# Batch 0 of a local-attention and token-mixing kernel: theta's weight jobs queued behind later softmax groups, half of the token weights queued behind theta, spare tiles and ScalarE steps for theta

## Chip, cores and metric

The kernel runs on one core of a Trainium2 chip. The metric is the device time of one launch in microseconds. The engines are TensorE (PE, with PEld for its weight loads), VectorE (DVE), ScalarE (ACT), GpSimd (POOL), and SyncE (SP), which issues all the transfers here.

## What is computed

For each of four batches (576 tokens, 8 heads of 64 channels):

```
scores = q @ k.T / 8, masked: head 0-3 see the last 32 tokens,
         head 4-7 see every 4th of the last 128
x      = softmax(scores) @ v                  # heads side by side: 576 x 512
theta  = x @ w_theta                          # 512 x 512
zr, zi = x * cos(theta), x * sin(theta)
u      = x + w_tok_r @ zr + w_tok_i @ zi      # mixes the 576 tokens
x2     = u + relu(u @ w_ch)
h      = relu(x2 @ w_in); hu, hv = halves of h
out    = (hu * (w_spatial @ layernorm(hv) + b)) @ w_out
```

Queries, keys and values come in single precision, all the weight matrices in double precision. A product of two single-precision matrices is computed as three passes of reduced-precision matmuls: each operand is split into a high part and the remainder (names ending in `h` and `l`), and high*high, low*high and high*low are added up.

## The kernel before

**Weights.** A weight piece comes in as 64-bit numbers, and the engines put together a single-precision value from them (`bits64`, lines 115 to 134): one scaling on ScalarE (L128) or POOL (L130), then three integer steps on DVE (L131 to L133). `split_weight` (L136) then writes the high part (L107 on ScalarE, L109 on DVE, L111 on POOL) and the remainder (L144, on POOL or DVE). There are four buffers for the 64-bit input (`w`) and four for the value (`w64g`). theta's weights are four jobs of two halves, all on POOL but for the DVE steps (`THETA_ENG`, L55; `w_theta_job`, L159). The token weights `wtok` have nine row blocks (k) and two column halves (c), so 18 jobs: half c=0 uses ScalarE, ScalarE and POOL, half c=1 POOL, POOL and DVE (`TOK_ENG`, L53).

**Attention.** One batch is 12 groups (`groups`, four head pairs of three). For a group, `att_scores` (L215) computes the scores, adds the mask on TensorE in batch 0 (L231), takes the maximum on DVE (L245 in batch 0; L249 and L250 in later batches), the exponentials on ScalarE (L253), one over their sum on DVE (L254, L255), and multiplies on POOL (L256). Two steps later `att_transpose` transposes the result, four steps later `att_values` multiplies with the values and ScalarE copies the result into `x`. The loads of all four head pairs of batch 0 are issued at its start (`att_load`, L195); the first two pairs of batch 1 are loaded behind the last transfer of token half c=0.

**Theta.** `th_unit` (L323) handles 128 tokens; the units of batch 0 run in the order 4, 0, 1, 2, 3 (unit 4 has the last 64 tokens). It scales and splits x on DVE (`xh` L335, `xl` L336), makes 12 matmuls (L341), rounds on ScalarE (`ta`, L345), subtracts on DVE (L346), transposes x (L349), takes the absolute value on DVE (`tb`, L350), two sines on ScalarE (L351, L352), two products with x on DVE (L355; L362 and L363 for unit 4), and splits each product: `zh` on DVE (L109) or POOL (L111), `zl` on POOL (L316). `ta` and `tb` have two buffers each, and unit 4's products use one of `ta`. A buffer comes free when POOL has read the product for `zl`.

**Mixing.** `tm_run` (L388) multiplies `z` by `wtok`, in 27 matmuls for each of four channel blocks and two token halves (column half c of `wtok`). The first two channel blocks of half c=0 are built up together, k by k, as the units of theta are done (L404); the rest at L411.

**Order.** Each engine carries out its instructions in order. A planner sets that order when the kernel is built: it goes by program order as the priority and by a model of when each instruction's operands are ready. The program order around the change is set by `spread`, which weaves jobs into a main sequence at a rate, and by `behind` (L480), which adds the rule that what a job issues on ScalarE, DVE and POOL comes after given instructions of the same engine. Before the change:

```
spread(attention(0), (jobs(j_theta), W_RATE0))
spread(th_run(0, (4, 0, 1, 2, 3)), (jobs([lambda f=f: behind(f) for f in j_tok0]), 2.0))
for b in range(PAIR):
    spread(chain(tm_run(b, K_ALL), take(ch, CH_BEFORE)), (attention(b + 1), ATT_RATE),
           (take(second, 12) if b else jobs(j_tok1 + j_ch), ...))
```

So theta's weight jobs are woven into attention of batch 0 with nothing that holds them; the jobs of token half c=0 are held behind the last softmax group of batch 0; the jobs of c=1 are written after theta and held by nothing; attention of batch 1 is woven into the mixing of batch 0.

Of the kernel before, what the change touches and what calls it, by code (L numbers as in the profile page):

```python
# [11 lines left out]
F32 = mybir.dt.float32  # L12
# [27 lines left out]


LAG_T, LAG_V = 2, 4
W_RATE0 = 0.5
TOK_RATE = 2.25
ATT_RATE, ATT_RATE_PAIR = 2.0, 3.0
TAIL_RATE = 1.0
# [16 lines left out]
def tile_block(ctx: ExitStack, tc: tile.TileContext, qT, kT, vw, eye_in, mask_in, eye_b_in, w_theta, w_tok, w_ch, w_in, w_sp, w_sph, b_sp, w_out, out):  # L63
# [3 lines left out]
    def f32(ap):  # L67
        return ap.bitcast(F32)
# [87 lines left out]
        split_weight(src[:, k, cs], t[:, 0], t[:, 1], *engs)  # L156
        SY.dma_start(f32(dst[:, k, :, cs]), f32(t))

    def w_theta_job(k):  # L159
        halves(w_theta, wth_h, wth_l, k, DM, THETA_ENG)  # L160

    def w_tok_job(k, c):
        cs = slice(CH * c, CH * (c + 1))
# [22 lines left out]
        for j in range(2):  # L186
            G.memset(qz[D * (1 - j):D * (2 - j), j], 0.0)

    last_softmax = {}
    tok0_dma = []  # L190
    groups = [(b, hp, g) for b in range(B) for hp in range(4) for g in range(3)]
    att = {}
# [2 lines left out]
    def att_load(b, hp):  # L195
        early = b == 0 and hp >= 2
        qz = qz_2[hp - 2] if early else qzero[hp % 2]
        kt = kt_2[:, hp - 2] if early else patt.tile([P, S + WIN], F32, tag="k", name="kt", bufs=2)
        first = b == 0 and hp == 0
        n = KW + (NA - 1) * T  # L200
        for c0, c1 in ((0, n), (n, S + WIN)) if first else ((0, S + WIN),):
            SY.dma_start(kt[:, c0:c1], kT[b, hp, :, c0:c1])
            if c0 == 0:
                SY.dma_start(qz[:D, 0], qT[b, hp, :D])
            if first and c0 == 0:
                SY.dma_start(masks, mask_in)
                SY.dma_start(eye_b, eye_b_in)
        SY.dma_start(qz[D:, 1], qT[b, hp, D:])
        if first:
            SY.dma_start(ident, eye_in)  # L210
        vt = vt_2[:KW, hp - 2] if early else patt.tile([KW, NT, P], F32, tag="v", name="vt", bufs=2)
        SY.dma_start(vt, vw[b, hp])
        heads[b, hp] = (qz, kt, vt, {})

    def att_scores(m):  # L215

        b, hp, g = groups[m]
        if g == 0 and (b or not hp):

            with tc.issue_after(tok0_dma[-1].ins) if b == 1 and hp < 2 else nullcontext():  # L220
                for h in range(1 if b else 4):
                    att_load(b, hp + h)
        if hp == 0 and g == 0:
            x[b] = p1.tile([P, 4, S], F32, tag="x", name=f"x{b}", bufs=2)
        qz, kt, vt, pT = heads[b, hp]
        s = ps_mm.tile([P, 512], F32, tag="mm", name="s")
        kind = 2 * (hp // 2) + g // 2
        on_pe = b < PE_MASK
        def mask_half(first):
            if on_pe:  # L230
                PE.matmul(s[:, :3 * KW], eye_b, masks[:, kind].rearrange("p t k -> p (t k)"), start=first, stop=not first)  # L231

        mask_half(True)
        for i in range(2 * 3):
            blk, h = i // 2, i % 2
            o = s[T * h:T * (h + 1), KW * blk:KW * (blk + 1)]
            j, t = (g, i) if g < 2 else (h, NA + blk)
            PE.matmul(o, qz[:, j, T * t:T * (t + 1)], kt[:, T * t:T * t + KW], start=not on_pe, stop=not on_pe)  # L238
        mask_half(False)
        sm = patt.tile([P, 3, KW], F32, tag="sm", name="sm", bufs=5)  # L240
        m_ = patt.tile([P, 3], F32, tag="m", name="m", bufs=3)
        l = patt.tile([P, 3], F32, tag="l", name="l", bufs=3)
        sv = s[:, :3 * KW].rearrange("p (t k) -> p t k", t=3)
        if on_pe:
            V.tensor_reduce(m_, sv, op=ALU.max, axis=AX.X, negate=True)  # L245
            A.mul(m_, m_, D**-0.5)
            src, scale = sv, D**-0.5
        else:
            V.scalar_tensor_tensor(sm, sv, D**-0.5, masks[:, kind], op0=ALU.mult, op1=ALU.add)  # L249
            V.tensor_reduce(m_, sm, op=ALU.max, axis=AX.X, negate=True)  # L250
            src, scale = sm, 1.0
        for t in range(3):
            ia = A.activation(sm[:, t, :], src[:, t, :], AF.Exp, bias=m_[:, t:t + 1], scale=scale, accum_out=l[:, t:t + 1])  # L253
        V.tensor_scalar_add(l, l, 1e-9)  # L254
        iv = V.reciprocal(l, l)  # L255
        ig = G.tensor_tensor(sm, sm, l.unsqueeze(2).to_broadcast([P, 3, KW]), op=ALU.mult)  # L256
        last_softmax[b] = (ia, iv, ig)
        att[m] = sm

    def att_transpose(m):  # L260
# [48 lines left out]


    zh, zl = {}, {}
    uu = {}

    def split(dst_h, dst_l, src, eh="a", el="g"):
        copy(dst_h, src, eh)
        (G if el == "g" else V).tensor_tensor(dst_l, src, f32(dst_h), op=ALU.subtract)  # L316

    def ztile(k, bufs=1):
        h = pz.tile([P, DM], F32R, tag=f"zh{k}", name=f"zh{k}", bufs=bufs)
# [3 lines left out]
    def th_unit(b, t, pair=False):  # L323
# [8 lines left out]
        h = pth.tile([P, 4, P], F32R, tag="xh", name="xh", bufs=2)[:, :, :n]  # L332
        l = pth.tile([P, 4, P], F32R, tag="xl", name="xl", bufs=2)[:, :, :n]

        V.tensor_scalar(h, src, INV2PI, None, op0=ALU.mult)  # L335
        V.scalar_tensor_tensor(l, src, INV2PI, f32(h), op0=ALU.mult, op1=ALU.subtract)  # L336
        ps = ps_mm.tile([P, 512], F32, tag="mm", name="ps_th")[:n]
        i = 0
        for k in range(4):
            for lh, rh in ((h, wth_h), (l, wth_h), (h, wth_l)):  # L340
                PE.matmul(ps, lh[:, k, :], rh[:, k, :], start=(i == 0), stop=(i == 11))  # L341
                i += 1
        ta = pth.tile([P, DM], F32, tag="ta", name="ta", bufs=2)[:n]
        tb = pth.tile([P, DM], F32, tag="tb", name="tb", bufs=2)[:n]
        A.activation(ta, ps, AF.Identity, bias=magic[:n, 0:1])  # L345
        V.scalar_tensor_tensor(ta, ta, MAGIC, ps, op0=ALU.subtract, op1=ALU.subtract)  # L346
        xn = ps_t.tile([P, 512], F32, tag="pt", name="ps_xn")[:n]
        for k in range(4):
            PE.transpose(xn[:, P * k:P * (k + 1)], src[:, k, :], ident)  # L349
        V.tensor_scalar(tb.bitcast(U32), ta.bitcast(U32), 0x7FFFFFFF, None, op0=ALU.bitwise_and)  # L350
        A.activation(ta, ta, AF.Sin, scale=-TURN)  # L351
        A.activation(tb, tb, AF.Sin, scale=-TURN, bias=half_pi[:n, 0:1])  # L352
        if t < 4:
            for k, tt in ((t, tb), (4 + t, ta)):
                V.tensor_tensor(tt, xn, tt, op=ALU.mult)  # L355
                zh[b, k], zl[b, k] = ztile(k)
                split(zh[b, k], zl[b, k], tt, Z_HI[k // 4], "g")
        else:
            for i in range(2 if pair else 1):
                r_ = slice(HALF * i, HALF * (i + 1))  # L360
                zz = pth.tile([P, DM], F32, tag=("ta", "tb")[i], name="zz", bufs=2)
                V.tensor_tensor(zz[:HALF], xn[r_], tb[r_], op=ALU.mult)  # L362
                V.tensor_tensor(zz[HALF:], xn[r_], ta[r_], op=ALU.mult)  # L363
                zh[b + i, 8], zl[b + i, 8] = ztile(8, 2)
                split(zh[b + i, 8], zl[b + i, 8], zz, "a", "g")

    xs = {}

    def th_keep(b):
# [86 lines left out]
    def jobs(fns):  # L456
        for f in fns:
            f()
            yield
# [6 lines left out]
        for g in gens:  # L466
            yield from g

    j_theta = [lambda k=k: w_theta_job(k) for k in range(4)]
    j_tok0 = [lambda k=k: w_tok_job(k, 0) for k in K_ALL]  # L470
    j_tok1 = [lambda k=k: w_tok_job(k, 1) for k in K_ALL]
    j_ch = [lambda k=k: w_ch_job(k) for k in range(4)]

    H2 = DM // 2
# [2 lines left out]
    j_out = [lambda k=k, c=c: stored(w_out, wo_d, k, slice(H2 * c, H2 * (c + 1)), OUT_ENG) for k in range(4) for c in range(2)]  # L477

    second = jobs(j_in + j_sp + j_out)
    def behind(f):  # L480

        with ExitStack() as st:
            for i in last_softmax[0]:
                st.enter_context(tc.issue_after(i.ins))
            f()
        tok0_dma.append(last_dma[0])

    spread(attention(0), (jobs(j_theta), W_RATE0))
    spread(th_run(0, (4, 0, 1, 2, 3)), (jobs([lambda f=f: behind(f) for f in j_tok0]), 2.0))
    for b in range(PAIR):  # L490
        ch = ch_run(b)
        spread(chain(tm_run(b, K_ALL), take(ch, CH_BEFORE)), (attention(b + 1), ATT_RATE), (take(second, 12) if b else jobs(j_tok1 + j_ch), 1.0 if b else TOK_RATE))
# [303 lines left out]
```

## Time and profile before

| | us |
|---|---|
| median of 3 runs | 570.19 |
| lowest and highest run | 569.38, 571.11 |
| the profiled execution | 569.31 |
| its span, first to last instruction | 567.5 |
| PE, PEld busy in the span | 534.8, 478.4 |
| DVE, ACT, POOL busy in the span | 331.0, 241.9, 262.1 |

The span is the profiled execution without what lies before its first and behind its last instruction. Busy times are of one execution. A wait is put down to the instruction that came last of those waited for. In a chain of waits each line has its start, its length and what it was. DVE's and ScalarE's instructions overlap a little at their ends, so a sum of durations is somewhat over the busy time of a stretch.

### The profile page before, as it was taken

What the parts mean: (1) busy time and instruction counts of PE and PEld (TensorE: products, weight loads), DVE (VectorE), ACT (ScalarE), POOL (GpSimd) and SP (SyncE); (2) the same over time, 40 slices, a digit from 0 to 9 for tenths busy, and PEclk for the clock granted to TensorE, in tenths of its full rate; (3) what the DMA queues carried; (4) which work ended last, traced back from release to release, by engine and by line L of the source; (5) the groups of instructions that cost most, each with busy time, mean ns of one, the idle gap of its engine ahead of it and who ended that gap; (6) DMA issues with size and microseconds to landing.
All of it is one profiled execution on the core that took longest, in us unless ns stands there. A gap on an engine that the chain in (4) does not pass through costs nothing.

```text
span 567.5 us, 11263 instructions
## 1 busy us (share of the span) xinstructions
PE 534.8 (94%) x4148; PEld 478.4 (84%) x4148; DVE 331.0 (58%) x844; ACT 241.9 (43%) x710; POOL 262.1 (46%) x333
## 2 busy tenths in 40 slices
PE   5887689999999999998899999999999999999997
PEld 3665578888988999877888999899899889988996
DVE  3589899898797269747697115773610327354030
ACT  3766476635655435766444212432322224223222
POOL 3484687552995348944349534334211203332040
PEclk9979799999999999999799999999999999999999
DMA  8845636672259453667400799705025110001002
GB/s 213 221 129 171 162 112 181 196 216 82 74 176 263 138 163 106 206 208 233 144 8 33 264 362 381 242 3 167 0 75 164 42 55 1 1 1 68 8 1 94
DMA packets 49935, 76.07 MB, mean 134 GB/s; under 512 B 4052, under 2 KB 30552, under 8 KB 49880
## 3 DMA queue, kind: packets, MB, share of 16 engines
q1 hardware_dynamic: 49880, 75.35, 43.3%
q8 instruction: 33, 0.54, 0.4%
q14 instruction: 22, 0.18, 0.1%
HBM read 52.53 MB, written 22.81 MB: 133 GB/s over the span
## 4 chain that ended last, share of the span: by engine, by line
PE 62%; DVE 10%; DMA 9%; POOL 7%; ACT 5%; issue 5%; SPq 1%; POOLq 0%; DVEq 0%; ACTq 0%
PE ps_y L411 12%; PE ps_sp L671 9%; PE ps_hu L652 9%; PE ps_o L700 9%; PE ps_hv L607 9%; PE ps_r L430 6%; POOL zl L316 2%; DMA wsp_d<-parts 2%; PE ps_th L341 2%; DMA w<-w_theta 1%; PE s L238 1%; DMA kt<-kT 1%; PE pt L266 1%; DVE xl L336 1%; DMA x2d<-parts 1%
## 5 line engine op out<-in xcount | busy, mean ns | idle before, releaser
L411 PE MATMUL ps_y<-wtok_h,zh 128*128 128x288 f32 x270 | 81.8, 306 | 1.7 <-DVE ta L346 0.9
L411 PE MATMUL ps_y<-wtok_h,zl 128*128 128x288 f32 x270 | 81.1, 301 | 0.4 <-POOL zl L316 0.4
L411 PE MATMUL ps_y<-wtok_l,zh 128*128 128x288 f32 x270 | 80.0, 298 | 0.0
L316 POOL TENSOR_TENSOR gl<-hu,gh 128x288 fp32r<-128x288 f32 x32 | 26.0, 811 | 74.6 <-ACT gh L107 74.6
L411 PEld LDWEIGHTS ps_y<-wtok_h,zh 128*128 128x128 f32 x270 | 50.7, 189 | 4.9 <-DVE sm L249 1.3
L675 DVE TENSOR_TENSOR hu<-ps_sp,hu 128x288 f32<-128x288 f32 x32 | 14.6, 455 | 66.8 <-PE ps_sp L674 66.8
L411 PEld LDWEIGHTS ps_y<-wtok_h,zl 128*128 128x128 f32 x270 | 51.0, 189 | 1.9 <-POOL zl L316 0.8
L411 PEld LDWEIGHTS ps_y<-wtok_l,zh 128*128 128x128 f32 x270 | 50.8, 189 | 0.2
L316 POOL TENSOR_TENSOR vl<-hv,vh 128x512 fp32r<-128x512 f32 x16 | 20.9, 1304 | 62.6 <-ACT vh L107 55.2
L256 POOL TENSOR_TENSOR sm<-sm,l 128x288 f32<-128x288 f32 x48 | 32.0, 673 | 31.6 <-DVE l L255 26.0
L253 ACT ACTIVATE sm<-sm,m 128x96 f32<-128x96 f32 x108 | 39.1, 364 | 13.4 <-DVE m L250 9.5
L316 POOL TENSOR_TENSOR ul<-x,uh 128x288 fp32r<-128x288 f32 x32 | 26.4, 832 | 25.2 <-ACT uh L107 25.1
L671 PE MATMUL ps_sp<-wsp_h,vh 128*128 128x288 f32 x128 | 37.8, 296 | 0.0
L430 PE MATMUL ps_r<-uh,wch_h 128*128 128x288 f32 x128 | 37.8, 296 | 0.0
L671 PE MATMUL ps_sp<-wsp_l,vh 128*128 128x288 f32 x128 | 37.8, 296 | 0.0
L671 PE MATMUL ps_sp<-wsp_h,vl 128*128 128x288 f32 x128 | 37.8, 295 | 0.0
L652 PE MATMUL ps_hu<-x2l,win_h 128*128 128x288 f32 x128 | 37.7, 295 | 0.0
L652 PE MATMUL ps_hu<-x2h,win_h 128*128 128x288 f32 x128 | 37.7, 295 | 0.0
L652 PE MATMUL ps_hu<-x2h,win_l 128*128 128x288 f32 x128 | 37.7, 295 | 0.0
L430 PE MATMUL ps_r<-uh,wch_l 128*128 128x288 f32 x128 | 37.7, 296 | 0.0
L316 POOL TENSOR_TENSOR parts<-x,parts 128x288 fp32r<-128x288 f32 x32 | 26.8, 844 | 23.4 <-ACT parts L107 23.4
L430 PE MATMUL ps_r<-ul,wch_h 128*128 128x288 f32 x128 | 37.4, 295 | 0.0
(169 smaller groups left out, 1590.9 us busy)
## 6 DMA issues: line engine op xcount, KB each, us to landing
x2d<-parts SPq DMA_DIRECT2D x32, 288.0 KB, 2.3
vt<-vw SPq DMA_DIRECT2D x16, 432.0 KB, 4.7
w<-w_tok SPq DMA_DIRECT2D x18, 288.0 KB, 2.8
x2h<-x2d SPq DMA_DIRECT2D x8, 576.0 KB, 7.7
x2l<-x2d SPq DMA_DIRECT2D x8, 576.0 KB, 10.9
kt<-kT SPq DMA_DIRECT2D x15, 304.0 KB, 4.5
w<-w_in SPq DMA_DIRECT2D x16, 256.0 KB, 3.5
win_d<-parts SPq DMA_DIRECT2D x16, 256.0 KB, 2.2
```

What stands on the lines that cost most here:

```text
L238: PE.matmul(o, qz[:, j, T * t:T * (t + 1)], kt[:, T * t:T * t + KW], start=not on_pe, stop=not on_pe)
L253: ia = A.activation(sm[:, t, :], src[:, t, :], AF.Exp, bias=m_[:, t:t + 1], scale=scale, accum_out=l[:, t:t + 1])
L256: ig = G.tensor_tensor(sm, sm, l.unsqueeze(2).to_broadcast([P, 3, KW]), op=ALU.mult)
L316: (G if el == "g" else V).tensor_tensor(dst_l, src, f32(dst_h), op=ALU.subtract)
L341: PE.matmul(ps, lh[:, k, :], rh[:, k, :], start=(i == 0), stop=(i == 11))
L411: PE.matmul(ps[:, :CH], lh[b, k][:, P * d:P * (d + 1)], rh[:, k, cs], start=(n == 0), stop=(n == 3 * len(ks) - 1))
L430: PE.matmul(ps[:, :CH], lh[:, k, P * e:P * (e + 1)], rh[:, k, cs], start=(n == 0), stop=(n == 11))
L607: PE.matmul(ps, lh[:, k, ts_], rh[:, k, DM:], start=(n == 0), stop=(n == 11))
L652: PE.matmul(ps[:, :CH], lh[:, k, fs], rh[:, k, cs], start=(n == 0), stop=(n == 11))
L671: PE.matmul(ps[:, :CH], lh[b, k][:, fs], rh[:, k, cs], start=(n == 0), stop=False)
L675: V.tensor_tensor(t[:, f, cs], ps[:, :CH], t[:, f, cs], op=ALU.mult)
L700: PE.matmul(ps, lh[:, k, ts_], rh[:, k, cs], start=(n == 0), stop=(n == 11))
```

## The change

- The masks of batch 0's first group come in a load of their own; the other three kinds follow behind the second half of the first queries.
- theta's weights become eight half jobs. Two are written after attention step 6, two after 7, one after 8, two after 9 and one after 10, and what each issues on ScalarE, DVE and POOL is queued behind that step's softmax.
- In batch 0, `xh` and the absolute value move from DVE to ScalarE.
- Units 0 and 1 of batch 0 use a spare tile for `ta` and `tb`, in the slot that held batch 0's early values and later holds `uh`.
- The nine jobs of token half c=1 are queued behind unit 3 of theta: behind its last sine on ScalarE, its last product on DVE and its last `zl` on POOL.

```diff
-W_RATE0 = 0.5
+TH_FROM, TH_RATE = 6, 6
...
-    def w_theta_job(k):
-        halves(w_theta, wth_h, wth_l, k, DM, THETA_ENG)
+    def w_theta_job(k, c):
+        cs = slice(DM // 2 * c, DM // 2 * (c + 1))
+        split_weight(w_theta[:, k, cs], wth_h[:, k, cs], wth_l[:, k, cs], *THETA_ENG)
...
-                SY.dma_start(masks, mask_in)
+                SY.dma_start(masks[:, :1], mask_in[:, :1])
                 SY.dma_start(eye_b, eye_b_in)
         SY.dma_start(qz[D:, 1], qT[b, hp, D:])
         if first:
+            SY.dma_start(masks[:, 1:], mask_in[:, 1:])
             SY.dma_start(ident, eye_in)
...
-        last_softmax[b] = (ia, iv, ig)
+        softmax[m] = (ia, iv, ig)
...
-        V.tensor_scalar(h, src, INV2PI, None, op0=ALU.mult)
+        if b == 0:
+            A.mul(h, src, INV2PI)
+        else:
+            V.tensor_scalar(h, src, INV2PI, None, op0=ALU.mult)
...
-        ta = pth.tile([P, DM], F32, tag="ta", name="ta", bufs=2)[:n]
-        tb = pth.tile([P, DM], F32, tag="tb", name="tb", bufs=2)[:n]
+        if b == 0 and t in (0, 1):
+            if not t:
+                spare.append(p1.tile([P, 4, DM], F32, tag="uh", name="spare"))
+            ta, tb = (spare[0][:, 2 * t + i, :] for i in range(2))
+        else:
+            ta, tb = (pth.tile([P, DM], F32, tag=g, name=g, bufs=2)[:n] for g in ("ta", "tb"))
...
-        V.tensor_scalar(tb.bitcast(U32), ta.bitcast(U32), 0x7FFFFFFF, None, op0=ALU.bitwise_and)
+        if b == 0:
+            A.activation(tb, ta, AF.Abs)
+        else:
+            V.tensor_scalar(tb.bitcast(U32), ta.bitcast(U32), 0x7FFFFFFF, None, op0=ALU.bitwise_and)
         A.activation(ta, ta, AF.Sin, scale=-TURN)
-        A.activation(tb, tb, AF.Sin, scale=-TURN, bias=half_pi[:n, 0:1])
+        ia = A.activation(tb, tb, AF.Sin, scale=-TURN, bias=half_pi[:n, 0:1])
...
-                V.tensor_tensor(tt, xn, tt, op=ALU.mult)
+                iv = V.tensor_tensor(tt, xn, tt, op=ALU.mult)
                 zh[b, k], zl[b, k] = ztile(k)
-                split(zh[b, k], zl[b, k], tt, Z_HI[k // 4], "g")
+                zlast[b] = ia, iv, split(zh[b, k], zl[b, k], tt, Z_HI[k // 4], "g")
...
-    spread(attention(0), (jobs(j_theta), W_RATE0))
-    spread(th_run(0, (4, 0, 1, 2, 3)), (jobs([lambda f=f: behind(f) for f in j_tok0]), 2.0))
+    for m, _ in enumerate(attention(0)):
+        for i in range(8):
+            if m == TH_FROM + TH_RATE * i // 10:
+                behind(softmax[m], lambda: w_theta_job(i // 2, i % 2))
+    s_last = softmax[11]
+
+    def tok0(k):
+        behind(s_last, lambda: w_tok_job(k, 0))
+        tok0_dma.append(last_dma[0])
+
+    spread(th_run(0, (4, 0, 1, 2, 3)), (jobs([lambda k=k: tok0(k) for k in K_ALL]), 2.0))
+    z_last = zlast[0]
+    j_tok1 = [lambda k=k: behind(z_last, lambda: w_tok_job(k, 1)) for k in K_ALL]
```

## Rows read from the trace of the kernel before

**Rows 1.** Busy time by stretch: PE, PEld, DVE, ACT, POOL, clock, DMA share, GB/s
```profile
0.00:7.00 7.00, 1.28 (x13) 1.03 (x13) 1.17 (x4) 1.28 (x1) 3.57 (x10) 1.00 0.61 169
7.00:24.00 17.00, 15.73 (x204) 10.98 (x203) 7.16 (x25) 12.19 (x68) 4.33 (x7) 1.00 1.01 262
24.00:38.00 14.00, 11.02 (x144) 8.33 (x143) 12.39 (x38) 8.57 (x37) 12.99 (x27) 0.76 0.50 137
38.00:78.00 40.00, 31.02 (x185) 24.24 (x185) 36.26 (x76) 24.00 (x50) 24.96 (x30) 0.91 0.57 154
70.30:78.00 7.70, 7.70 (x76) 7.14 (x77) 7.70 (x18) 7.61 (x18) 6.81 (x10) 0.96 0.49 132
82.00:121.00 39.00, 39.00 (x427) 35.07 (x428) 36.62 (x107) 22.64 (x86) 25.73 (x42) 1.00 0.67 189
```

**Rows 2.** Chain that ended last, 50 to 82 us: start, length, what
```profile
56.06 5.65 DMA w<-w_tok
...
69.87 0.69 ACT ta L345
...
73.39 1.28 ACT L351
```

**Rows 3.** Timeline of DVE and POOL, 58 to 101 us: start, length, what
```profile
61.86 0.44 POOL L130 TENSOR_SCALAR w64g<-w 128x288 f32<-128x288 f32 x1 [2.10 <-DMA w<-w_tok]
...
70.66 0.45 DVE L131 TENSOR_SCALAR c<-w 128x288 uint32<-128x288 uint32 x1
...
77.31 0.68 DVE L355 TENSOR_TENSOR ta<-ps_xn,ta 128x512 f32<-128x512 f32 x1
...
100.85 0.45 DVE L144 TENSOR_TENSOR wtok_l<-w64g,wtok_h 128x288 fp32r<-128x288 f32 x1
```

**Rows 4.** ACT's groups, 38 to 78 us: busy us, mean ns, idle before
```profile
L128 ACT ACTIVATE w64g<-w 128x288 f32<-128x288 f32 x9 | 4.1, 471 | 7.4 <-POOL wtok_l L144 3.3 <-POOL wth_l L144 1.7 <-DMA w<-w_tok 1.2
...
L345 ACT ACTIVATE ta<-ps_th,magic 128x512 f32<-128x512 f32 (+1 forms) x5 | 3.4, 684 | 6.7 <-POOL zl L316 6.6
L351 ACT ACTIVATE ta<-ta 128x512 f32<-128x512 f32 (+1 forms) x5 | 3.2, 631 | 1.7 <-DVE tb L350 1.7
...
L253 ACT ACT_TABLE_LOAD x2 | 2.6, 1283 | 0.0
L253 ACT ACTIVATE sm<-sm,m 128x96 f32<-128x96 f32 x6 | 2.2, 365 | 0.0
L253 ACT ACTIVATION_READ_ACCUMULATOR sm<-sm,m 128x1 f32 x5 | 0.9, 186 | 0.0
```

**Rows 5.** DVE's groups, 38 to 78 us: busy us, mean ns, idle before
```profile
L346 DVE SCALAR_TENSOR_TENSOR ta<-ta,ps_th 128x512 f32<-128x512 f32 (+1 forms) x5 | 3.4, 676 | 2.2 <-ACT ta L345 2.2
...
L350 DVE TENSOR_SCALAR tb<-ta 128x512 uint32<-128x512 uint32 (+1 forms) x5 | 2.6, 525 | 0.0
L335 DVE TENSOR_SCALAR xh<-x 128x512 fp32r<-128x512 f32 (+1 forms) x5 | 2.5, 535 | 0.8 <-ACT x L296 0.8
```

**Rows 6.** Timeline of SP, first 7 us: start, length, what
```profile
1.80 0.58 SPq L206 DMA_DIRECT2D masks<-mask  x1
```

**Rows 7.** Who waited for whom, 7 to 24 us: total us, times, longest
```profile
POOL w64g L130 <- DMA w<-w_theta: 3.9, 1, 3.9
DVE c L131 <- DMA w<-w_theta: 2.7, 1, 2.7
```

**Rows 8.** DVE's groups, 70.6 to 101.4 us: busy us, mean ns, idle before
```profile
L350 DVE TENSOR_SCALAR tb<-ta 128x512 uint32<-128x512 uint32 x1 | 1.0, 977 | 0.0
L346 DVE SCALAR_TENSOR_TENSOR ta<-ta,ps_th 128x512 f32<-128x512 f32 x1 | 0.7, 679 | 0.0
L355 DVE TENSOR_TENSOR ta<-ps_xn,ta 128x512 f32<-128x512 f32 x1 | 0.7, 676 | 0.0
L355 DVE TENSOR_TENSOR tb<-ps_xn,tb 128x512 f32<-128x512 f32 x1 | 0.7, 654 | 0.0
L109 DVE CAST zh<-tb 128x512 fp32r<-128x512 f32 x1 | 0.4, 414 | 0.0
```

More of the change, by code (lines that the diff above doesn't have):

```diff
@@ L187, in tile_block @@
             G.memset(qz[D * (1 - j):D * (2 - j), j], 0.0)
-    last_softmax = {}
+    softmax = {}
     tok0_dma = []
@@ L311, in tile_block @@
     zh, zl = {}, {}
+    zlast = {}
     uu = {}
@@ L315, in split @@
         copy(dst_h, src, eh)
-        (G if el == "g" else V).tensor_tensor(dst_l, src, f32(dst_h), op=ALU.subtract)
+        return (G if el == "g" else V).tensor_tensor(dst_l, src, f32(dst_h), op=ALU.subtract)
     def ztile(k, bufs=1):
@@ L365, in th_unit @@
                 split(zh[b + i, 8], zl[b + i, 8], zz, "a", "g")
+    spare = []
     xs = {}
@@ L467, in chain @@
             yield from g
-    j_theta = [lambda k=k: w_theta_job(k) for k in range(4)]
-    j_tok0 = [lambda k=k: w_tok_job(k, 0) for k in K_ALL]
-    j_tok1 = [lambda k=k: w_tok_job(k, 1) for k in K_ALL]
     j_ch = [lambda k=k: w_ch_job(k) for k in range(4)]
@@ L479, in tile_block, with behind @@
     second = jobs(j_in + j_sp + j_out)
-    def behind(f):
+    def behind(ins, f):
         with ExitStack() as st:
-            for i in last_softmax[0]:
+            for i in ins:
                 st.enter_context(tc.issue_after(i.ins))
             f()
+    for m, _ in enumerate(attention(0)):
[5 more added lines that the diff above has]
+        behind(s_last, lambda: w_tok_job(k, 0))
         tok0_dma.append(last_dma[0])
-    spread(attention(0), (jobs(j_theta), W_RATE0))
-    spread(th_run(0, (4, 0, 1, 2, 3)), (jobs([lambda f=f: behind(f) for f in j_tok0]), 2.0))
+    spread(th_run(0, (4, 0, 1, 2, 3)), (jobs([lambda k=k: tok0(k) for k in K_ALL]), 2.0))
+    z_last = zlast[0]
+    j_tok1 = [lambda k=k: behind(z_last, lambda: w_tok_job(k, 1)) for k in K_ALL]
     for b in range(PAIR):
```

## The prediction

> **What bounds the kernel now.** I read the busy time by stretch first [rows 1]. The reader is to see four stages. From 7 to 24 us the DMA engines are full (share 1.01) and the vector engines mostly wait: the queries, keys and values of batch 0 are arriving. From 24 to 38 us DVE (12.39 of 14 us) and POOL (12.99) are full: the last softmax groups and theta's weights. From 38 to 78 us, batch 0's theta with the first half of the token weights, DVE is full again (36.26 of 40) while TensorE idles 9 us and runs at a mean granted clock of 0.91, so part of it at the lower of its levels of 1.2 and 2.4 GHz. From 82 to 121 us TensorE never stops and DVE has 36.62 of 39 us. So the only stretch that can give time back is the one before 82 us, and whatever the change pushes behind it meets a full TensorE and a nearly full DVE.
>
> Then the chain of waits inside that stretch [rows 2]. It goes from a transfer of token weights of 5.65 us into POOL's first conversion step of the *second* token half (L130 at 61.86, [rows 3]), from there through POOL's queue to ScalarE's L345 at 69.87, and on over a read of ScalarE's table at 73.39. Two faults show. POOL, in order, stands behind a second-half job that theta does not need; and ScalarE's L345 of units 2 and 3 waits 6.6 us in all for POOL's zl (idle column of [rows 4]), because `ta` has two buffers and the one wanted is still read by POOL. DVE in turn stands 2.2 us before its L346 [rows 5].
>
> **The change part by part.** All in the profiled execution's own time, 569.31 us, which lies 0.88 us under the 570.19 us median of the runs shown.
>
> *Masks in two loads.* 72 of 288 KB now go ahead of the small identity for which TensorE's first matmul waits. At 169 GB/s [rows 1] the 221 kB moved back are worth at most 1.3 us; one more issue on SP costs at most the 0.58 us of the present one [rows 6]. I take nothing: the transfers are full from 7 to 24 us, the bytes are the same, and the last of them set the end of that stage. The third group needs the moved part, which comes behind the query half that the group waits for as well.
>
> *Theta's weights behind softmax groups 6 to 10.* The same eight half jobs, so no engine gains work. Now POOL stands 3.9 us and DVE 2.7 us for the first theta weight [rows 7] with softmax work queued behind them. The constraint puts only group 6 ahead of the first two jobs; the job's transfer lands no earlier, because SP issues it behind the same loads, so both engines stand at the next job instead and groups 7 to 11 still queue there. What moves into the gap is one POOL multiply and two short DVE steps, under 1 us. The stage from 24 to 38 us is full on both engines [rows 1]. Bounds: 0 and the whole DVE stand of 2.7 us; I take 0, the nearer by the order.
>
> *ScalarE takes xh and the absolute value.* Five units each: DVE loses 2.5 us (L335, the scaled copy xh) and 2.6 us (L350, the absolute value) [rows 5], 5.1 us. ScalarE gains ten steps. The nearest rows are its own 512-wide ones, 684 and 631 ns [rows 4]: ten times 0.66 is 6.6 us. DVE's L350 and L335 took 0.53 us, so a unit's own latency grows by about 0.25 us; over a pipeline of five units that shows once or twice, under 0.5 us.
>
> The Trainium skill speaks against this part (page "ScalarE: Activation LUTs", section "Rules for kernel authors"): multiplications and the like belong on VectorE, which is faster. The rows agree on the single step (0.53 against 0.66 us); whether it decides here is the second rival below.
>
> *Spare tiles for units 0 and 1.* They remove the wait for POOL's zl: 6.6 us of ScalarE, of which 2.2 us stood on DVE. What is late next is the unit's product with x on DVE, that is, DVE's own queue. The spare space is the slot of batch 0's early value tiles, which attention has read before theta begins, and POOL's last reading of it (unit 1) lies ahead of unit 3, so it is free before the first mixed column is written into that slot; no wait from it.
>
> *Second token half behind theta.* It removes POOL's L130 from in front of zh and 2.1 us of standing there [rows 3]. Nine jobs wait behind unit 3's last product on DVE and last subtraction on POOL; ScalarE has none of their steps. Their transfers are not held, except that the fifth waits for a buffer that the first job frees. That job's first DVE step is at 70.66 now [rows 3], so SP, with the next batch's later loads behind it, is not held longer unless theta ends after that.
>
> **The sum.** When does theta's last DVE product end? Now at 78.0 [rows 3]. From 38 to 78 us DVE is busy 36.26. Away go 5.1 us (moved). Between 70.3 and 78 us DVE is busy all 7.70 us [rows 1], of which unit 3's own steps are 0.98 + 0.68 + 0.65 + 0.68 = 3.0 us [rows 8]; the other 4.7 us, second-half weights and the next batch's softmax, go behind theta. That leaves 26.5 us. With the 3.7 us of idle time of now, the end comes at 38 + 26.5 + 3.7 = 68.2. Dense it would be 64.5; with twice the idle time, since fill work has left DVE, 72.0.
>
> What is that worth? DVE delivers the nine second-half weights from 70.66 to 101.3 us [rows 3], 30.6 us, and TensorE's second column half is woven around them. In these 30.6 us lie 3.4 us of unit 3 (3.0 us and L109's 0.41 [rows 8]). Started on a DVE free of theta they need 27.2 us, so a start at 74.1 us would change nothing, and a start at 68.2 brings everything after it forward by **5.9 us** (9.6 dense, 2.1 with twice the idle). TensorE can follow: it has 9 us of idle time before 78 us and slow stretches besides. After 121 us I expect the same work, shifted. So 563.4 us in profiled time, and 564.3 us as a median of runs.
>
> **Rivals.**
> *Stage one pays too.* If the order that the planner finds leaves groups 7 and 8 ahead of the first theta weight, the 2.7 us that DVE stands there become useful: 561.6 us. For it: the work is ready by then. Against: only group 6 is forced ahead. Chance 0.12.
>
> *ScalarE takes DVE's place.* From 38 to 78 us it is busy 24.0 us [rows 1]; without the next batch's exponentials (2.2 us), their accumulator reads (0.9) and table reads (2.6) [rows 4], and without the Sin table read again at 73.39 (1.28) [rows 2], 7.0 us together, and with 6.6 us added, it has 23.6 us, near DVE's 26.5. Its idle time before L128 (7.4 us, for POOL, mostly) and before L351 (1.7 us) [rows 4] remains, and the moved xh now queues behind that L128. Then the last product ends at 38 + 23.6 + 9.1 + 1.3 = 72.0 us and 2.1 us are gained: 568.1, close to the limit of what can be told. Chance 0.16, of which 0.09 falls under that limit. The rule of the Trainium skill named above, taken as deciding, gives this case.
>
> *The second half comes too late* (the slower side). If theta still ends at 78 us, since five units hand over between ScalarE, DVE and POOL many times and the fill work is gone, the weights start at 78 instead of 70.66 and the last arrives at 78 + 27.2 = 105.2 instead of 101.3; TensorE, which has no idle time there, stands 3.9 us: 574.1 us. It decides from a theta end after 74.1 us. For it: DVE is never idle from 70 to 78 us, and the fill hides latency now. Against: the two long waits in the chain go. Chance 0.13.
>
> *The absolute value calls a table.* No row shows that function on ScalarE. If it evicted Sin, each of five units would read a table twice more, ten times 1.283 us [rows 4]: 12.8 us on top of the second rival, 581 us. Against: from 38 to 78 us ScalarE mixes copies, scaled copies and the biased identity with Sin, and reads a table for Sin and the exponentials alone. Chance 0.03. The Trainium skill ("ScalarE: Activation LUTs", section "Table sets: the hidden batching unit") says that copy, identity and the absolute value are in every set; the rows agree for the first two, and none shows the third.
>
> **How the numbers follow.** The forecast has chance 0.56 and 560.6 to 568.1 us (theta's end at 64.5 and 72). The measurement tells 0.3%, 1.7 us, from no change. Faster: 0.56 + 0.12 + 0.07 = 0.75. Same: 0.09. Slower: 0.13 + 0.03 = 0.16. The range runs from 558.5 us (stage one pays on top of an almost dense theta) to 571 us (the second rival and the beginning of the third).
>
> **What the changed profile would show.** Right: L335 and L350 gone from DVE in batch 0, ScalarE's wait for POOL's zl near zero, no L130 of 288 columns on POOL before the last zl, theta's last product near 68 us, the last second-half weight near 95 us, TensorE dense from about 70 us. The last two Exp and Sin reads of table inside theta should be gone or one pair fewer. Wrong: theta's last product after 74 us; TensorE standing at L411 for wtok_l; ScalarE the busiest engine from 38 to 70 us; or extra table reads beside the absolute value. If theta ends near 68 us and the time stays, the gain was lost after 82 us, where DVE has the deferred 4.7 us to make up and less than 2.4 us of slack in 39.

## The result and the profile after

The changed kernel takes **563.69 us** (median of 4 runs, 560.85 to 564.04); the kernel before, timed beside it, 570.65 us (569.38 to 571.32). The ratio is 0.987, with a 95% interval of 0.9833 to 0.9907. The forecast was 564.3 us. The time is right; the way to it, as the runs below show, is only partly the one that the prediction named.

The head of the changed kernel's page: busy time of the engines, TensorE's busy tenths and its granted clock in 40 slices.

```profile
PE 535.4 (95%) x4148; PEld 477.2 (85%) x4148; DVE 323.7 (58%) x834; ACT 245.6 (44%) x718; POOL 261.7 (47%) x333
PE   4987999999999999996999999999999999999997
PEclk9899999999999999998899999999999999999999
```

The span is 562.2 us (before 567.5). TensorE is busy as long as before (535.4 against 534.8 us). What is gone is time in which it does nothing: 567.5 - 534.8 = 32.7 us before, 562.2 - 535.4 = 26.8 us after, 5.9 us less. These two numbers, **TensorE's busy time and its idle time, which add up to the span**, are followed through all the runs below.

The changed kernel's busy time by stretch, columns as in [rows 1]:

```profile
0.00:7.00 7.00, 2.25 (x17) 1.32 (x19) 1.45 (x5) 1.28 (x1) 3.57 (x10) 1.00 0.60 153
7.00:24.00 17.00, 13.60 (x160) 9.72 (x160) 6.47 (x24) 10.36 (x58) 4.34 (x7) 0.80 1.00 236
24.00:38.00 14.00, 13.31 (x189) 9.77 (x187) 11.96 (x37) 12.18 (x52) 12.67 (x26) 1.00 0.58 169
38.00:78.00 40.00, 33.44 (x233) 26.63 (x232) 37.12 (x84) 30.30 (x81) 29.11 (x36) 1.00 0.63 169
82.00:121.00 39.00, 39.00 (x399) 33.75 (x396) 33.20 (x95) 19.84 (x72) 21.77 (x35) 1.00 0.62 180
```

Against [rows 1] the reader is to see four things. From 38 to 78 us TensorE works 2.4 us more (31.02 to 33.44) and its clock is 1.00 instead of 0.91. DVE is no emptier there (36.26 to 37.12): what it no longer does for theta is filled with other work. ScalarE gains 6.3 us (24.00 to 30.30); 12 more exponentials of the next batch lie in this stretch than before (18 against 6), and two table reads fewer (2 against 4). And the first 24 us got worse for TensorE (17.01 to 15.85 us busy, clock 1.00 to 0.80 from 7 to 24), which the stretch from 24 to 38 makes up (11.02 to 13.31).

The changed kernel's timeline of DVE and POOL: theta's last product, its last `zl`, the first steps of a second-half job, the last second-half weight. They answer to [rows 3].

```profile
66.11 0.67 DVE L368 TENSOR_TENSOR ta<-ps_xn,ta 128x512 f32<-128x512 f32 x1
71.62 1.29 POOL L319 TENSOR_TENSOR zl<-ta,zh 128x512 fp32r<-128x512 f32 x1
72.87 0.87 POOL L130 TENSOR_SCALAR w64g<-w 128x288 f32<-128x288 f32 x2
73.46 0.45 DVE L131 TENSOR_SCALAR c<-w 128x288 uint32<-128x288 uint32 x1
99.31 0.45 DVE L144 TENSOR_TENSOR wtok_l<-w64g,wtok_h 128x288 fp32r<-128x288 f32 x1
```

Theta's last product ends at 66.78 us (before 77.99). But the second half starts on DVE only at 73.46 (before 70.66), since POOL's L130 comes behind the last `zl`, and its last weight comes at 99.31, only 1.5 us sooner than before.

ScalarE's groups from 38 to 78 us in the changed kernel (busy us, mean ns, idle before), to be read against [rows 4]:

```profile
L128 ACT ACTIVATE w64g<-w 128x288 f32<-128x288 f32 x9 | 4.2, 467 | 4.8 <-DMA w<-w_tok 4.2 <-POOL wth_l L144 0.6
L355 ACT ACTIVATE ta<-ps_th,magic 128x512 f32<-128x512 f32 (+1 forms) x3 | 2.0, 681 | 0.0
L361 ACT ACTIVATE tb<-ta 128x512 f32<-128x512 f32 (+1 forms) x3 | 1.9, 632 | 0.1
L339 ACT ACTIVATE xh<-x 128x512 fp32r<-128x512 f32 x3 | 1.9, 628 | 0.0
L364 ACT ACT_TABLE_LOAD x1 | 1.3, 1283 | 0.0
L255 ACT ACT_TABLE_LOAD x1 | 1.3, 1283 | 0.0
```

L355 (L345 before) no longer waits: 6.7 us of idle time are 0.0. The absolute value (L361) and the scaled copy (L339) take 0.63 us each.

**Where the time was.** The prediction had read that ScalarE's L345 waits for POOL's `zl`. It had not read that TensorE waits for the next `zl` behind it. The kernel before, 56 to 72 us: who waited for whom, and, from the timeline, TensorE's instruction at the end of its wait:

```profile
ACT ta L345 <- POOL zl L316: 6.1, 2, 4.6
PE ps_y L404 <- POOL zl L316: 4.4, 1, 4.4
```

```profile
65.83 0.61 PE L404 MATMUL ps_y<-wtok_h,zl 128*128 128x288 f32 x1 [4.41 <-POOL zl L316]
```

And the same stretch by 3 us in the kernel before, then in the changed one (columns as in [rows 1]):

```profile
60.00:63.00 3.00, 1.14 (x6) 0.72 (x6) 3.00 (x8) 0.03 (x1) 1.14 (x2) 1.00 1.05 244
63.00:66.00 3.00, 0.17 (x1) 0.17 (x2) 0.79 (x3) 1.01 (x2) 2.92 (x4) 0.67 0.55 145
66.00:69.00 3.00, 3.00 (x12) 2.73 (x12) 2.93 (x7) 1.57 (x3) 3.00 (x4) 0.50 0.16 29
69.00:72.00 3.00, 3.00 (x24) 2.77 (x24) 2.83 (x8) 2.11 (x3) 3.00 (x5) 0.69 0.21 75
```

```profile
60.00:63.00 3.00, 3.00 (x32) 2.39 (x30) 3.00 (x7) 2.89 (x6) 3.00 (x4) 1.00 1.08 256
63.00:66.00 3.00, 2.04 (x30) 1.73 (x29) 3.00 (x8) 2.97 (x9) 3.00 (x4) 1.00 1.02 232
66.00:69.00 3.00, 3.00 (x25) 3.00 (x24) 3.00 (x8) 1.40 (x7) 3.00 (x4) 1.00 0.94 225
```

Before, TensorE works 1.31 of the 6 us from 60 to 66; then the granted clock is at 0.50 (1.2 GHz) although it works without a break. Unit 0's two `zl`, late behind L130 [rows 3], thus stop ScalarE and TensorE together, and the slow clock comes on top. Of TensorE's 4.41 us, POOL's stand for the transfer and L130 itself are at most 2.5 (2.10 and 0.44, [rows 3]).

From 121 us on nothing more is gained. Before to after, the first `uh` of batch 0 comes 5.5 us sooner (86.4 to 80.9), the last theta matmul 5.4 us (296.7 to 291.3), the last matmul of the channel product 5.3 us (356.4 to 351.1), the end of the span 5.3 us.

### The profile page after: what moved, and what is told of

Same layout as the page of the kernel before. It is cut to its first block, busy times and chain, and to the rows that moved or that the text cites. A ratio compares the mean times of both kernels' runs of the same rounds, so it can differ in the third digit from the quotient of the medians.

```text
span 562.2 us, 11265 instructions
## 1 busy us (share of the span) xinstructions
PE 535.4 (95%) x4148; PEld 477.2 (85%) x4148; DVE 323.7 (58%) x834; ACT 245.6 (44%) x718; POOL 261.7 (47%) x333
## 4 chain that ended last, share of the span: by engine, by line
PE 63%; DVE 11%; DMA 8%; POOL 6%; ACT 5%; issue 5%; SPq 1%; POOLq 0%; DVEq 0%; ACTq 0%
PE ps_y L425 12%; PE ps_sp L693 9%; PE ps_hu L674 9%; PE ps_o L722 9%; PE ps_hv L629 9%; PE ps_r L444 5%; PE s L240 3%; DMA wsp_d<-parts 2%; PE pt L268 2%; DMA win_d<-parts 2%; POOL zl L319 2%; PE ps_x L282 2%; POOL parts L144 1%; DMA qz<-qT 1%; DMA x2d<-parts 1%
## 5 line engine op out<-in xcount | busy, mean ns | idle before, releaser
L258 POOL TENSOR_TENSOR sm<-sm,l 128x288 f32<-128x288 f32 x48 | 32.6, 680 | 27.4 <-DVE l L257 22.1
L240 PE MATMUL s<-kt,qz 128*64 128x96 f32 x504 | 35.5, 268 | 4.6 <-DMA qz<-qT 3.4
```

## The experiments

Each is one edit of the changed kernel, or one or more parts of the change put into the kernel before. Each of the twelve had 5 rounds beside the kernel before.

**Masks in one load again.**

```diff
-                SY.dma_start(masks[:, :1], mask_in[:, :1])
+                SY.dma_start(masks, mask_in)
...
-            SY.dma_start(masks[:, 1:], mask_in[:, 1:])
```

> The changed kernel with the masks in one load again. Theory A (the forecast: the split load is worth nothing): within 1.7 us of the changed kernel's 563.7 us, theta's last product on DVE within 1.5 us of 66.8 us. Theory B (the earlier first matmul is where stage one's gain comes from): the first matmul back at 5.7 us, x of batch 0 complete about 1 us later than the 37.0 us of the changed kernel, 565 us. Theory C (the moved masks delay the second pair's queries, for which TensorE stood 3.4 us): that wait goes, TensorE's clock does not fall from 7 to 24 us, and the time is 561 to 562 us.

Measured: 563.73 us, ratio 0.9874 (0.9847 to 0.9901). In the full change this part is worth nothing, as the prediction had it.

**Second token half not held.**

```diff
-    j_tok1 = [lambda k=k: behind(z_last, lambda: w_tok_job(k, 1)) for k in K_ALL]
+    j_tok1 = [lambda k=k: w_tok_job(k, 1) for k in K_ALL]
```

> The changed kernel without the hold of the second token half. Theory A (the forecast: the hold clears POOL for theta): second-half L130 steps stand in front of zh and zl again, theta's last product on DVE moves from 66.8 to 69 us or later, and the time rises by 2 to 3 us, to about 566. Theory B (the hold is worth nothing, because the other parts had already cleared the waits): the last second-half weight comes earlier than 99.8 us by 2 us or more, theta's end stays within 1.5 us, and the time stays within 1.7 us of 563.7.

Measured: 562.88 us, 0.9864 (0.983 to 0.9897). The hold is not what gains; without it the kernel is no slower, and 0.8 us faster in the median, which these intervals can't tell from nothing.

**No spare tiles.**

```diff
-        if b == 0 and t in (0, 1):
+        if False:
```

> The changed kernel with two buffers for ta and tb in all units. Theory A (the forecast, with theta's end passed on one for one): ScalarE waits 4 to 6 us for POOL's zl again, theta's last product comes at 71 to 73 us, and the time is 568 to 569 us. Theory B (what counts is TensorE's idle time before 82 us, and theta's end is passed on only in part): the same wait and the same late product, but the time rises by no more than 2 us, to 565 or 566, as TensorE has batch 1's scores and the early matmuls to do meanwhile.

Measured: 569.42 us, 0.9989 (0.9971 to 1.0008). All of the gain is gone with this one part. The waits from 56 to 72 us in this run:

```profile
ACT ta L355 <- POOL zl L319: 2.8, 2, 2.2
...
PE ps_y L418 <- POOL zl L319: 1.2, 1, 1.2
```

Both waits for `zl` are back, though shorter than before. They are not all: TensorE's idle time in this stretch is 4.61 us (5.42 before, 0.96 with the full change), and its longest wait there, 1.7 us, is for a product of DVE. Whether that one too goes back to the late `zl` was not followed.

**xh and the absolute value back on DVE.**

```diff
-        if b == 0:
+        if False:
             A.mul(h, src, INV2PI)
...
-        if b == 0:
+        if False:
             A.activation(tb, ta, AF.Abs)
```

> The changed kernel with xh and the absolute value on DVE again. Theory A (the forecast: DVE bounds theta, 5.1 us less work on it): theta's last product on DVE moves from 66.8 us to 70 to 72 us and the time rises by 3 to 5 us, to 567 to 568. Theory B (with spare tiles and the hold, DVE has room, and ScalarE and POOL set the pace): theta's end moves by less than 1.5 us and the time stays within 1.7 us of 563.7.

Measured: 568.33 us, 0.997 (0.9949 to 0.9991): 4.6 us given back. Yet theta's last product starts at 65.98 us, as early as with the full change, so its end is not what decides. In the profiled execution TensorE's idle time is as low as with the full change (27.1 us); its busy time is 5.6 us higher (541.0 us), and three stretches before 82 us run at the lower clock:

```profile
33.00:36.00 3.00, 3.00 (x37) 2.48 (x36) 1.92 (x5) 1.52 (x5) 3.00 (x6) 0.50 0.63 186
...
48.00:51.00 3.00, 3.00 (x9) 2.28 (x9) 2.31 (x6) 2.92 (x5) 0.09 (x1) 0.53 0.00 0
...
66.00:69.00 3.00, 2.01 (x17) 1.80 (x16) 3.00 (x9) 1.61 (x8) 2.97 (x5) 0.50 1.04 230
```

That execution took 570.01 us, at a mean granted clock of 0.979. Ten of the twelve executions of this kernel had 0.984 to 0.991, about the full change's 0.987 to 0.991, and still a median of 568.25 us. So the clock is not what the 4.6 us are, and where they lie in such an execution is not shown.

**The kernel before with the spare tiles alone.** The edit is the `if b == 0 and t in (0, 1):` block of the diff, and nothing else.

> The kernel before with the spare tiles alone. Taken out of the changed kernel alone (the run e3) they cost 5.7 us. Theory A (the parts' effects add): ScalarE's wait for POOL's zl goes and the time falls by 4 to 6 us, to 564 to 566. Theory B (each part shortens one of two limits that lie side by side, so both are needed): the wait goes, but DVE still carries the 5.1 us of xh and absolute value, the last first-half weight comes no earlier, and the time is 568 to 570 us.

Measured: 564.89 us, 0.9903 (0.9879 to 0.9928), 5.2 us faster than the kernel before. In its trace POOL and DVE show:

```profile
56.87 1.27 POOL L318 TENSOR_TENSOR zl<-spare,zh 128x512 fp32r<-128x512 f32 x1
...
69.06 0.63 POOL L130 TENSOR_SCALAR w64g<-w 128x288 f32<-128x288 f32 x1
```

```profile
105.29 0.91 DVE L144 TENSOR_TENSOR wtok_l<-w64g,wtok_h 128x288 fp32r<-128x288 f32 x1
```

Unit 0's first `zl` comes at 56.87 us (63.29 before, behind L130's stand for a transfer), and the first second-half L130 only at 69.06, with no hold at all: the planned order is another. So the run shows what the spare tiles and the order that comes with them are worth, and does not tell the two apart. No wait of ScalarE or of a matmul for `zl` is left from 38 to 82 us. And the last second-half weight comes **4.4 us later** than before (105.29 against 100.85, [rows 3]) in a kernel that is 5.2 us faster.

**The kernel before with ScalarE's steps alone** (the two `if b == 0:` blocks of the diff).

> The kernel before with xh and the absolute value on ScalarE alone. Taken out of the changed kernel alone (the run e4) they cost 4.6 us. Theory A (effects add): 564 to 566 us. Theory B (both parts needed): ScalarE, in order, still waits for POOL's zl, and now xh of the later units stands behind that wait; theta's last product stays near 78 us and the time is 569 to 571 us.

Measured: 568.65 us, 0.9974 (0.9958 to 0.9989). DVE's last second-half weight:

```profile
96.09 0.46 DVE L144 TENSOR_TENSOR wtok_l<-w64g,wtok_h 128x288 fp32r<-128x288 f32 x1
```

This is the earliest weight of all the runs, 4.8 us ahead of the kernel before, near the 95 us that the prediction wanted, and the whole edit is worth 1.4 us. With the run above, the link from the weights to the time is refuted from both sides.

**The kernel before with both.**

> The kernel before with the spare tiles and the ScalarE steps, without the split masks, the hold of theta's weights and the hold of the second token half. Theory A (the forecast: the hold of the second half is needed as well, since its L130 stands in front of zh on POOL): 565 to 567 us. Theory B (these two parts are the whole change): within 1.7 us of the changed kernel's 563.7, theta's last product within 2 us of 66.8 us.

Measured: 564.61 us, 0.9896 (0.9864 to 0.9927). On top of the spare tiles ScalarE's steps are worth 0.3 us, less than the measurement tells.

**Second half later still.** In the changed kernel the nine jobs are put behind a softmax group of batch 1, three empty slots later, at a higher rate.

```diff
-TOK_RATE = 2.25
+TOK_RATE = 3.0
...
-    j_tok1 = [lambda k=k: behind(z_last, lambda: w_tok_job(k, 1)) for k in K_ALL]
+    j_tok1 = [lambda: None] * 3 + [lambda k=k: behind(softmax[15], lambda: w_tok_job(k, 1)) for k in K_ALL]
```

> The changed kernel with the second token half held behind batch 1's softmax group 3 and written after three idle slots (the channel weights keep their distance through a rate of 3 in place of 2.25), so that its first POOL step comes at about 77 us, 4 us later than the 72.9 us of the changed kernel. Theory A (the forecast's link: the nine second-half weights pace what follows): the last of them comes at about 104 us in place of 99.8 and the time rises by 3 to 4 us, to 567 to 568. Theory B (TensorE's lost time ahead of the dense stretch decides, and these weights have slack): the last weight as late, the time within 1.7 us of 563.7.

Measured: 564.99 us, 0.9899 (0.9874 to 0.9923), 1.3 us over the changed kernel, less than can be told. POOL's first second-half L130 starts at 75.85 us, 3.0 later than in the changed kernel, and the last weight at 101.62 us, 2.3 later; 4 us were planned. A rise of 1.3 us for 2.3 us of delay does not tell the link from slack. That the weights have slack rests on the runs with the spare tiles alone and ScalarE's steps alone.

Three runs then asked why taking ScalarE's steps away costs 4.6 us although adding them to the spare tiles gains 0.3.

**The kernel before with the spare tiles and the hold of the second half.** The lines of the hold, beside those that collect `zlast`:

```diff
+    z_last = zlast[0]
+    j_tok1 = [lambda k=k: behind(z_last, lambda: w_tok_job(k, 1)) for k in K_ALL]
```

> The kernel before with two parts alone: the spare tiles and the hold of the second token half. Spare tiles alone gave 564.9 us, the full change without ScalarE's steps 568.3. Theory A (the hold costs some 3 us as long as DVE keeps xh and the absolute value, since it pushes the nine second-half jobs behind a later theta): 567.5 to 569, last second-half weight near 107 us. Rival B (the hold is worth nothing either way; what cost 3.4 us is the order that the planner finds in the first 24 us with masks and theta's weights moved): 564 to 566.

Measured: 567.44 us, 0.9968 (0.9946 to 0.999). Theory A's range begins at 567.5, and its weight near 107 us is there (107.43): the hold costs 2.5 us where DVE keeps its steps. In the profiled execution it is idle time: TensorE's is 33.4 us, against 27.8 with the spare tiles alone, at the same busy time (534.8). That execution, 569.98 us, is the longest of the twelve, so a part of the 5.6 us is its own.

**Spare tiles, masks and theta's weights** (the changed kernel without ScalarE's steps and without the hold).

> The changed kernel without ScalarE's steps and without the hold of the second half, that is, spare tiles, masks in two loads and theta's weights behind the softmax groups. Theory A (it is the hold that costs, when DVE keeps its steps): 564 to 566. Rival B (it is masks and theta's weights that cost): 567.5 to 569. If neither this one nor the spare tiles with the hold alone is above 567, the 3.4 us need both and no single part is to blame.

Measured: 568.89 us, 0.9983 (0.996 to 1.0006). This is in rival B's range, so both theories about met their numbers: the hold costs by itself, and so does what moves in the first 24 us, and the two together (568.3 us) cost no more than the second alone.

**The hold alone.**

> The kernel before with the hold of the second token half alone. The prediction's third rival says that with theta ending at 78 us the hold makes the last second-half weight come at 105.2 us and the time 574 us. Theory A: 572 to 575. Rival B (the weights have slack, as the run with the hold moved to the next batch's softmax showed): 569 to 571, with the last weight at 104 us or later all the same.

Measured: 575.41 us, 1.0097 (1.006 to 1.0135), the only run that is slower than the kernel before, and a little above theory A's range. That is near the 574.1 us of the prediction's third rival, but not by its mechanism. TensorE never stands from 82 to 121 us:

```profile
82.00:100.00 18.00, 18.00 (x197) 15.69 (x196) 17.86 (x49) 10.82 (x44) 11.58 (x21) 1.00 0.65 180
100.00:121.00 21.00, 21.00 (x216) 18.47 (x217) 18.90 (x54) 11.73 (x42) 11.57 (x18) 1.00 0.67 195
```

In the profiled execution TensorE's idle time over the whole span is lower than before (31.0 against 32.7 us) and its busy time 6.0 us higher (540.8), at a mean granted clock of 0.975 against 0.982; between 160 and 200 us it is 0.91 on the mean, where it was 1.00 before. But the clock differs between executions of one kernel: it is 0.973 to 0.979 in the six of this one and 0.973 to 0.982 in the 23 of the kernel before beside them, and those of the 23 with 0.975 or 0.976 took 569.75 to 573.68 us, a median of 570.8. So the clock is a small part of the 5.7 us at most, and where the rest lies is not shown.

The hold does take L130 out of unit 0's way, and TensorE's waits for `zl` fall from 4.4 to 2.5 us:

```profile
PE ps_y L417 <- POOL zl L318: 2.5, 2, 1.8
```

The kernel is slower all the same, so a shorter wait for `zl` is not enough by itself.

**Spare tiles and theta's weights** (as two runs above, but with the masks in one load).

> The kernel before with the spare tiles and theta's weights behind the softmax groups, masks in one load. With the masks in two loads as well it took 568.9 us, with the spare tiles alone 564.9. If the two mask loads cost that difference, 564 to 566; if theta's weights do, 567.5 to 569. Theory: the two mask loads, since with them TensorE idles for queries at 9 to 12 us, and the granted clock falls to half in the first 24 us; in the runs with one mask load it stays at 1.00 there. So 564 to 566, with clock 1.00 from 0 to 24 us.

Measured: 564.8 us, 0.9905 (0.9882 to 0.9927), the same as the spare tiles alone, as the theory had it, and the clock stays at 1.00 from 0 to 24 us. So theta's weights are worth nothing, and in this company it is the two mask loads, with the order that comes with them, that cost 4.1 us. Three stretches with two mask loads (two runs above), then with one (this run), columns as in [rows 1]:

```profile
9.00:12.00 3.00, 1.02 (x15) 0.57 (x11) 1.05 (x5) 2.53 (x14) 1.33 (x2) 1.00 1.06 242
12.00:15.00 3.00, 2.61 (x22) 2.01 (x24) 0.71 (x3) 0.39 (x2) 0.14 (x1) 0.58 1.03 248
...
33.00:36.00 3.00, 2.91 (x49) 2.13 (x45) 2.39 (x6) 2.38 (x10) 3.00 (x7) 1.00 0.62 176
```

```profile
9.00:12.00 3.00, 3.00 (x28) 1.84 (x25) 1.26 (x4) 1.55 (x10) 0.67 (x1) 1.00 1.05 253
12.00:15.00 3.00, 3.00 (x44) 2.21 (x39) 2.08 (x8) 2.02 (x13) 0.84 (x2) 1.00 1.05 251
...
33.00:36.00 3.00, 3.00 (x41) 2.46 (x40) 1.91 (x5) 1.53 (x6) 3.00 (x7) 0.50 0.69 189
```

With two loads TensorE works 1.02 of 3 us from 9 to 12 instead of all 3.00, and its clock is 0.58 behind that. But this does not explain the 4.1 us: with one load the low clock comes later instead, 0.50 from 33 to 39 us, where with two it is 1.00.

All runs side by side, in us. Starts, busy, idle and clock are of the one profiled execution of each, which lies up to 2.9 us on either side of the median; the mean clock of one kernel differs from execution to execution (kernel before: 0.973 to 0.987 in the 74 beside the twelve runs).

| kernel | median | start of theta's last product | start of last second-half weight | TensorE idle | TensorE busy | clock |
|---|---|---|---|---|---|---|
| before | 570.2 | 77.31 | 100.85 | 32.7 | 534.8 | 0.982 |
| full change | 563.7 | 66.11 | 99.31 | 26.8 | 535.4 | 0.987 |
| - masks | 563.7 | 69.65 | 101.59 | 26.1 | 537.6 | 0.979 |
| - hold | 562.9 | 65.96 | 98.02 | 27.5 | 532.8 | 0.988 |
| - spare tiles | 569.4 | 78.08 | 107.00 | 31.9 | 537.5 | 0.981 |
| - ScalarE's steps | 568.3 | 65.98 | 104.18 | 27.1 | 541.0 | 0.979 |
| later hold | 565.0 | 65.72 | 101.62 | 27.4 | 535.8 | 0.988 |
| spare alone | 564.9 | 72.98 | 105.29 | 27.8 | 534.8 | 0.988 |
| ScalarE's steps alone | 568.7 | 75.52 | 96.09 | 31.8 | 535.9 | 0.985 |
| spare + ScalarE's steps | 564.6 | 69.74 | 99.06 | 27.4 | 538.2 | 0.978 |
| spare + hold | 567.4 | 73.79 | 107.43 | 33.4 | 534.8 | 0.988 |
| spare + masks + theta's weights | 568.9 | 65.88 | 103.61 | 29.0 | 537.8 | 0.988 |
| hold alone | 575.4 | 74.21 | 102.54 | 31.0 | 540.8 | 0.975 |
| spare + theta's weights | 564.8 | 65.28 | 99.85 | 26.1 | 534.0 | 0.988 |

Two columns fail to order the medians: theta's last product starts within 0.7 us in kernels of 562.9, 564.8 and 568.9 us, and the last weight at 105.29 goes with 564.9, at 96.09 with 568.7. The idle column falls into two groups: with the spare tiles it is 26 to 29 us (but for the one with the hold on DVE's full load, 33.4); without them 31 to 33. Within a group it does not order the medians either: 27.1 us go with 568.3, 27.8 with 564.9.

What a part is worth, by what it is added to (difference of two medians; "alone" is against the kernel before as timed beside that run, 570.06 us, for the hold 569.74). Each median is known to some 1.5 us, so a difference of two variants to some 2 us:

| part | alone | on top of | in the full change |
|---|---|---|---|
| spare tiles | -5.2 | -4.0 (ScalarE's steps) | -5.7 |
| ScalarE's steps | -1.4 | -0.3 (spare) | -4.6 |
| hold of the second half | +5.7 | +2.5 (spare) | +0.8 |
| masks in two loads | not run | +4.1 (spare, theta's weights) | 0.0 |
| theta's weights | not run | -0.1 (spare) | not run |

## Why the prediction was right, and where it was not

**Masks, taken at nothing:** right in the full change (0.0). Its reason, that the bytes are the same and the last of them set the end of the stage, left out what TensorE does meanwhile: the clock from 7 to 24 us fell from 1.00 to 0.80, and rose from 0.76 to 1.00 from 24 to 38 us. Without ScalarE's steps and the hold that part costs 4.1 us, more than the bounds allowed for.

**Theta's weights, taken at nothing:** right (564.8 against 564.9 us with the spare tiles). Within the full change the run was not made; there, taking this hold out swaps one POOL multiply in the planned order and nothing else. The first rival, that stage one pays too, is seen by halves: TensorE works 2.3 us more from 24 to 38 us and 1.2 us less before.

**ScalarE's steps:** the term was right (0.63 us a step for a forecast 0.66, so ten make 6.3 us for 6.6). That ScalarE's busy time from 38 to 78 us also grew by 6.3 us is chance: only eight of the ten steps lie there, with the 12 more exponentials and the two table reads fewer. DVE's 5.1 us bought little by themselves: alone 1.4 us, on the spare tiles 0.3. They are worth 4.6 us only beside the masks and the hold, which hurt while DVE carries those steps; why, is not shown, since executions at the full change's clock lose as much.

The second rival, ScalarE as the bound, did not come: theta's last product ended at 66.78 us and not at 72.0, and from 38 to 70 us ScalarE was busy 25.4 us, DVE 29.4. The rule of the Trainium skill ("ScalarE: Activation LUTs", section "Rules for kernel authors") that multiplications belong on VectorE holds for the single step here (0.53 us on DVE, 0.63 on ScalarE), and does not decide the time of this kernel.

The fourth rival is out as well. From 38 to 78 us ScalarE reads a table once for Sin and once for an exponential (before, twice each), and none beside the absolute value. The Trainium skill ("ScalarE: Activation LUTs", section "Table sets: the hidden batching unit") says that this function is in every set; the trace agrees, and it is the row that was missing.

**Spare tiles:** the wait of 6.6 us was read rightly (6.1 of it are units 2 and 3, the rest unit 1) and it went to 0.0. The step mis-sized its consequence: it was counted as ScalarE's time with 2.2 us on DVE, one part among three. It is the whole gain as near as can be told (alone 5.2 of 6.5 us, and without it 569.4). The traces point to the reason: the same `zl` also stopped TensorE for 4.41 us, with the clock at 0.50 behind it, and with the spare tiles alone neither is left from 56 to 72 us (the clock is 1.00 there). How much of that is the buffers and how much the new order was not separated. The chain of waits [rows 2] follows one path and did not show TensorE's share; the list of waits of that stretch does, and the prediction had read the groups of ScalarE and DVE alone there [rows 4, 5].

**Hold of the second half:** it removes L130 from in front of `zh`, as said, but the spare tiles alone do this too. By itself it costs 5.7 us, though TensorE's wait for `zl` gets shorter.

**The sum.** Theta's last DVE product was forecast to end at 68.2 us and ended at 66.78; up to there from 38 us DVE was busy 26.2 us (forecast 26.5) and idle 2.6 (3.7). That step held, and it was not the one that counted. **The step that failed is the link**: "a start at 68.2 brings everything after it forward by 5.9 us", with the second-half weights as what hands it on. By that sum, the start at 73.46 us, behind POOL's last `zl` rather than DVE's last product, would have given 74.1 - 73.46 = 0.6 us. The time fell by 6.5 us in the comparison's medians (5.3 in the profiled spans) all the same. The weights have slack, and in this pair of profiles what passes on is the time that TensorE loses before 82 us: 20.45 us of idle time up to 121 us before, 15.39 after, 5.1 of the 5.3 us. That 5.9 us were forecast and about that came is luck, a coincidence of two sizes: the failed link and the true cause both go back to the same late `zl`.

**The third rival** gave 574.1 us for a hold with theta still late. The hold alone, theta ending at 74.9 us, took 575.4, but TensorE never waited from 82 to 121 us, so the price was met by another road, which stays open.

**Open.** Why two mask loads cost 4.1 us in one company and nothing in another was not settled, nor why taking ScalarE's steps away costs 4.6 us. Almost every variant also moves hundreds of instructions in the planner's order, so a part's worth here is that of the part with the order that comes with it. No variant beats the full change by more than the measurement tells; the one without the hold (562.9 us) is the shortest.

## What to carry to other kernels

Before following a queue of work to the end, split the span of the engine that bounds the kernel into busy and idle time, and ask of each of its longest waits which single instruction ends it: here one late pair of subtractions on POOL stopped ScalarE by its buffer and TensorE by its data, and two more buffers, with the order that came with them, gave 5.2 of the change's 6.5 us. Holding work back so that something else may go first is a gain only if the held work has slack and the engine that it leaves has something else to do; the same hold cost 5.7, 2.5 and 0.8 us in three companies, the last too small to tell from nothing. A single profile is one execution: before a loss is put down to the clock, compare the clock of all the executions. Parts of a change that a planner reorders do not add up, so test each both alone and taken out.

## What the runs showed of the hardware

TensorE's granted clock fell to 0.50 (1.2 GHz) behind stretches in which it had little to do: after 1.31 busy us of 6 in the kernel before (60 to 66 us), after 0.58 of 3 in the changed one (9 to 12 us; 0.50 from 12 to 18). It was at 0.50 and 0.69 from 66 to 72 us in the kernel before, where TensorE was busy without a break. Matmuls of one shape in that run, at the lower clock and at the higher one:

```profile
66.48 0.44 PE L404 MATMUL ps_y<-wtok_h,zl 128*128 128x288 f32 x1
66.72 0.44 PE L404 MATMUL ps_y<-wtok_l,zh 128*128 128x288 f32 x1
...
71.39 0.29 PE L404 MATMUL ps_y<-wtok_h,zl 128*128 128x288 f32 x1
71.52 0.29 PE L404 MATMUL ps_y<-wtok_l,zh 128*128 128x288 f32 x1
```

They start 0.24 us apart in the first pair and 0.13 us in the second. So time that TensorE stands can be paid for again when it resumes.

That is not the measure of a kernel, though: the mean clock differs between executions of one kernel, and the kernel without ScalarE's steps was 4.6 us slower than the full change with a clock of 0.984 to 0.991 in ten of its twelve executions, against 0.987 to 0.991 in the full change's four.
